# An attention-and-MLP block on one core: the front part laid out anew before the main loop

## The chip, the core and the metric

The kernel runs on one core of a Trainium2 chip, as one launch. The metric is the device time of that launch in microseconds. The engines are called as the profile calls them: PE (matrix products), DVE, ACT and POOL (elementwise work), SP (which here only issues transfers). PEld is PE's loading of weights.

## The reference, cut to what matters

```python
x = A_x                                               # 1 x 2048 x 512
mod = (silu(c) @ w_mod).reshape(1, 6, 1, 512)         # sa, ca, ga, sb, cb, gb
h = layernorm(x) * (1 + ca) + sa
q = (h @ wq), 32 heads of 16;  k = h @ wk;  v = h @ wv    # one key and value head for all
o = softmax(q @ k.T / 4) @ v
x = x + ga * (o @ wo)
h = layernorm(x) * (1 + cb) + sb
x = x + gb * (gelu(h @ w1 + b1) @ w2 + b2)            # 512 -> 1376 -> 512
```

## The kernel before, in words

**Two parts.** A front part loads x in four blocks of 512 rows, normalizes and modulates them, turns them so that features lie along partitions (the tiles h0 and big1 to big3, each as a high and a low part whose sum is the full number), and makes the keys and values of all 2048 rows. The main loop then runs over 64 units; a unit is 256 rows times 4 heads. For each unit the loop makes the scores of all keys (tile `e`, line 596), their exponentials on ACT (tile `p`, line 597) and the products with the values (tile `acc`, line 608). It also does, in pieces between these, the query projections of later groups, the output projection and the MLP.

**Maxima.** The softmax of a unit needs the maximum of each row of scores first. For this a score product `m` (line 516) of 128 rows times 512 keys goes into one of three PSUM banks, and DVE reduces it to one column of `mx` (line 521). A unit has 32 of them: key block kc 0 to 3, head pair j 0 or 1, row half t 0 or 1, and side s 0 or 1. The side says which half of PE's 128 rows the product uses: s = 0 the rows 0 to 63, s = 1 the rows 64 to 127. In the listings below a product is called m, then the unit, then j_t_kc_s. When the last maximum of a unit is in, `put_max` reduces the key blocks (tile `mm`, line 570), turns the result (`turned`, line 571), gathers it into `mt` (line 565), splits it into `mh` and `ml` and sends these with transfers (line 560) into two rows of the unit's query tile `qst`. Only then can the scores `e` of that unit be made. The maxima run ahead of the loop: those of unit 0 all come in the front part, with some of unit 1.

**What sets the order.** Every engine's order is written out by hand: the program is recorded in the order in which the Python code calls the operations. In the front part that order is the table `SLOTS`. Each row first does a number of maxima (`chunk`), then single steps of named jobs: "keys b" is three of the twelve products of the keys and values of block b (tile `kps`, line 163), and its fourth step also copies them out on ACT (`kv_out`, lines 391 and 392); "low b" is the low part of the keys on DVE (line 397); "k b" repeats them on ACT (line 401); "heads b" turns one quarter of block b (four transposes, tile `tp`, line 370) and modulates it; "v b" turns the values (tile `vps`); "q 1" is three products of the second query group (tile `qps`); "rows" is eight small products for the late modulation (tile `modl`); "wq g" splits the weights of query group g; "load" fetches the queries of unit 2. `FIRST_MAX` says in which order unit and key block of the first two units come, `LEAD_0` how many maxima (32 + 4 * LEAD_0) are done when the loop is entered. From there `lead` spreads what is left evenly over the first eight units.

**Transfers.** Query tiles go to DRAM (`send_q`) and come back into `qst` by four transfers for each unit (`load_q`, lines 486 and 487), all on SP's queue.

Of the kernel before, what the change touches and what calls it, by code (L numbers as in the profile page):

```python
# [22 lines left out]
LEAD_0 = 6  # L23
FIRST_MAX = ((0, 0), (1, 0), (0, 1), (1, 1), (0, 2), (0, 3), (1, 2), (1, 3))
SLOTS = ((4, "keys 1", "keys 1"), (2, "keys 1", "keys 1"), (2, "low 1", "heads 2"), (2, "heads 2", "k 1"), (2, "heads 2"), (2, "heads 2", "v 0"),
# [22 lines left out]
def raw(ap):  # L48
    return ap.bitcast(F32)
# [3 lines left out]
def adaln_mqa_mlp(  # L53
# [273 lines left out]
    def prep_wq(g):  # L327
        gs = slice(g * P, (g + 1) * P)
        for j in range(2):
# [3 lines left out]
            nc.scalar.copy(dh, src)  # L333
            nc.gpsimd.tensor_tensor(out=dl, in0=src, in1=raw(dh), op=ALU.subtract)
# [95 lines left out]
    def qproj(b, g):  # L430

        ps = psum.tile([P, BQ], F32, name=f"qps{b}_{g}", tag="v" if g else "x")
# [41 lines left out]
    def load_q(u):  # L474
# [7 lines left out]

        for s in (1, 0):
# [53 lines left out]
    def put_max(u, mx):  # L537
# [17 lines left out]
        def send():  # L555
            for s in (1, 0):
                for r, src in ((48, mh), (49, ml)):
                    dst = qst[64 * s + r:64 * s + r + 1].rearrange("p j (t n) -> p (j t) n", n=P)
                    ring = nc.scalar if u == 0 and s else nc.sync
# [3 lines left out]
        def gather():  # L563
            for g in range(0, P, 32):
                nc.gpsimd.tensor_scalar(out=mt[:, g:g + 32], in0=turned[g:g + 4 * T, :], scalar1=1.0, scalar2=0.0,  # L565
                                        op0=ALU.mult, op1=ALU.add)
            split(mh, ml, mt, nc.gpsimd, nc.gpsimd)
# [644 lines left out]
    def chunk(n):  # L1212
        for _ in range(n):
            mp.step(mp.done % 2)
# [53 lines left out]
    def one(fn, *args):  # L1268
        fn(*args)
        yield  # L1270
# [22 lines left out]
    def first_q(t):  # L1293
        if t == 1:
            run(q_group())
            load_q(0)
            load_q(1)
# [9 lines left out]

    def last_h(t):
        if t == QT - 1:
            run(h1)  # L1310
# [3 lines left out]
    repeat_k(0)  # L1314
    run(xhat1(2, act))
    run(xhat1(3, act))
    work = {"keys 1": keys(1), "heads 2": heads(2), "heads 3": heads(3), "q 1": q_group(), "keys 2": keys(2), "keys 3": keys(3),
# [215 lines left out]
```

## Time and profile before

| what | value |
|---|---|
| median of 3 runs | 1579.92 us (1579.86 to 1580.32) |
| the profiled execution | 1579.71 us, its span 1577.9 us |
| mean granted clock of PE | 0.997 |
| PE busy | 1554.7 us (99%) |
| DVE busy | 1403.8 us (89%) |
| ACT busy | 1204.3 us (76%) |
| POOL busy | 695.3 us (44%) |
| first score product `m` starts | 34.13 us |
| maxima of unit 0 complete (`mm` starts) | 74.03 us |
| first scores of the loop (`e` starts) | 79.75 us |

Times in the trace count from the start of the span. In a row of the timeline the first number is the start, the second the length, then engine, line and operation with its tiles; in brackets stands how long the engine idled before it and what the trace names as the end of that idle time. A row of the table by stretches gives the busy time and the number of instructions of PE, PEld, DVE, ACT and POOL, the granted clock of PE, and the transfers' share and rate.

### The profile page before, as it was taken

What the parts mean: (1) busy time and instruction counts of PE and PEld (TensorE: products, weight loads), DVE (VectorE), ACT (ScalarE), POOL (GpSimd) and SP (SyncE); (2) the same over time, 40 slices, a digit from 0 to 9 for tenths busy, and PEclk for the clock granted to TensorE, in tenths of its full rate; (3) what the DMA queues carried; (4) which work ended last, traced back from release to release, by engine and by line L of the source; (5) the groups of instructions that cost most, each with busy time, mean ns of one, the idle gap of its engine ahead of it and who ended that gap; (6) DMA issues with size and microseconds to landing.
All of it is one profiled execution on the core that took longest, in us unless ns stands there. A gap on an engine that the chain in (4) does not pass through costs nothing.

```text
span 1577.9 us, 43469 instructions
## 1 busy us (share of the span) xinstructions
PE 1554.7 (99%) x17506; PEld 1040.3 (66%) x17506; DVE 1403.8 (89%) x2491; ACT 1204.3 (76%) x2418; POOL 695.3 (44%) x1253
## 2 busy tenths in 40 slices
PE   5999999999999999999999999999999999999999
PEld 3466655667767676667766677676766677676767
DVE  6899999999999999999999999999999999999715
ACT  5477777788877887778877887778877788778863
POOL 4345447447422472245523463334712465224731
PEclk8999999999999999999999999999999999999999
DMA  7236323313021120312112130212112030221341
GB/s 250 83 110 203 121 81 91 100 36 105 20 61 63 59 82 22 93 33 94 46 44 83 44 99 19 76 48 86 56 32 93 27 107 31 62 76 49 100 141 54
DMA packets 80858, 121.48 MB, mean 77 GB/s; under 512 B 16186, under 2 KB 55354, under 8 KB 80400
## 3 DMA queue, kind: packets, MB, share of 16 engines
q1 hardware_dynamic: 80640, 118.70, 23.2%
q8 instruction: 137, 2.24, 0.6%
q14 instruction: 65, 0.53, 0.1%
q10 hardware_dynamic: 16, 0.00, 0.0%
HBM read 91.00 MB, written 26.88 MB: 75 GB/s over the span
## 4 chain that ended last, share of the span: by engine, by line
PE 95%; ACT 3%; DVE 1%; DMA 0%; issue 0%; POOL 0%; SPq 0%; ACTq 0%; DVEq 0%
PE acc L608 32%; PE e L596 20%; PE m L516 18%; PE w1ps L192 8%; PE w2ps L192 6%; PE wops L192 3%; PE qps L192 2%; ACT p L597 2%; PE w2ps L186 1%; PE w1ps L186 1%; PE tp L192 1%; DVE mx L521 1%; PE kps L163 1%; PE wops L186 0%; PE modr L288 0%; DMA xt<-in_A_x_dram 0%
## 5 line engine op out<-in xcount | busy, mean ns | idle before, releaser
L521 DVE TENSOR_REDUCE mx<-m 128x1 f32<-128x512 f32 x2048 | 1270.6, 681 | 98.9 <-PE m L516 90.3
L597 ACT ACTIVATE p<-e 128x512 f32<-128x512 f32 x2048 | 1067.1, 601 | 290.5 <-PE e L596 200.2
L516 PE MATMUL m<-ks,qst 64*128 64x512 f32 x2048 | 828.4, 431 | 6.4 <-DVE ve L204 4.9
L596 PE MATMUL e<-qst,ks 64*128 64x512 f32 x2048 | 731.5, 412 | 2.1 <-ACT wqH L333 1.3
L608 PE MATMUL acc<-p,va 128*32 128x256 f32 x8192 | 548.3, 385 | 0.0
L516 PEld LDWEIGHTS m<-ks,qst 64*128 64x128 f32 x2048 | 367.2, 184 | 103.4 <-DVE mx L521 82.2
L596 PEld LDWEIGHTS e<-qst,ks 64*128 64x128 f32 x2048 | 357.6, 184 | 112.6 <-ACT p L597 102.0
L608 PEld LDWEIGHTS acc<-p,va 128*32 128x32 f32 x8192 | 214.2, 109 | 216.9 <-issue 113.2
L192 PE MATMUL w1ps<-h2H,w1t 64*128 64x256 f32 x1232 | 236.1, 288 | 0.0
L192 PEld LDWEIGHTS w1ps<-h2H,w1t 64*128 64x128 f32 x1232 | 184.0, 185 | 31.7 <-issue 22.2
L565 POOL TENSOR_SCALAR mt<-turned 8x32 f32<-8x32 f32 x256 | 53.2, 208 | 339.0 <-DVE turned L571 326.9
L192 PE MATMUL w1ps<-h2L,w1t 64*128 64x256 f32 x616 | 169.3, 275 | 0.0
L192 PE MATMUL w2ps<-w2H,gH 64*128 64x256 f32 (+1 forms) x556 | 162.3, 296 | 0.0
L192 PE MATMUL w2ps<-w2L,gH 64*128 64x256 f32 (+1 forms) x556 | 156.6, 283 | 0.0
L192 PE MATMUL w2ps<-w2H,gL 64*128 64x256 f32 (+1 forms) x556 | 155.1, 283 | 0.0
L192 PEld LDWEIGHTS w1ps<-h2L,w1t 64*128 64x128 f32 x616 | 113.5, 184 | 0.0
L192 PEld LDWEIGHTS w2ps<-w2H,gH 64*128 64x128 f32 x556 | 101.6, 184 | 10.8 <-issue 4.9
L192 PEld LDWEIGHTS w2ps<-w2H,gL 64*128 64x128 f32 x556 | 101.8, 184 | 2.3
L192 PEld LDWEIGHTS w2ps<-w2L,gH 64*128 64x128 f32 x556 | 102.4, 184 | 1.4
L957 POOL TENSOR_SCALAR tt<-tt 128x256 f32<-128x256 f32 x77 | 31.0, 403 | 144.8 <-ACT tt L956 144.8
L192 PE MATMUL wops<-woH,onH 64*128 64x256 f32 x224 | 67.8, 303 | 0.0
L192 PE MATMUL wops<-woL,onH 64*128 64x256 f32 x224 | 62.2, 277 | 0.0
(233 smaller groups left out, 1602.7 us busy)
## 6 DMA issues: line engine op xcount, KB each, us to landing
w1t<-dw SPq DMA_DIRECT2D x82, 512.0 KB
qst<-dq SPq DMA_DIRECT2D x128, 64.0 KB
do<-oc SPq DMA_DIRECT2D x63, 128.0 KB
dw<-w1s SPq DMA_DIRECT2D x11, 512.0 KB
xt<-in_A_x_dram SPq DMA_DIRECT2D x4, 1024.0 KB
dq<-qH SPq DMA_DIRECT2D x16, 256.0 KB
dq<-qL SPq DMA_DIRECT2D x16, 256.0 KB
qst<-dq SPq DMA_DIRECT2D x128, 32.0 KB
```

What stands on the lines that cost most here:

```text
L163: nc.tensor.matmul(ps, a, b_, start=begin and n == 0, stop=end and n == last)
L186: nc.tensor.matmul(ps, a, b_, start=first_, stop=last_)
L192: nc.tensor.matmul(ps, a[rows], b_[rows], start=first_ and s == begin, stop=last_ and s != begin)
L516: nc.tensor.matmul(m, qsts[u][rows, j, t * P:(t + 1) * P], ks[rows, kc * 512:(kc + 1) * 512], start=True, stop=True)
L521: nc.vector.tensor_reduce(out=self.mx[u][:, i, kc:kc + 1], in_=m, axis=AX.X, op=ALU.max)
L565: nc.gpsimd.tensor_scalar(out=mt[:, g:g + 32], in0=turned[g:g + 4 * T, :], scalar1=1.0, scalar2=0.0, op0=ALU.mult, op1=ALU.add)
L596: nc.tensor.matmul(e, ks[rows, kt * P:(kt + 1) * P], rhs, start=True, stop=True)
L597: nc.scalar.activation(ptiles[u, K][:, j, s, :], e, AF.Exp, scale=0.25)
L608: ins = nc.tensor.matmul(accs[u][32 * cidx:32 * cidx + 32, :], va[:, kt, :], rhs, start=kt == 0, stop=kt == NKT - 1)
L957: nc.gpsimd.tensor_scalar(out=tt, in0=tt, scalar1=1.0, scalar2=1.0, op0=ALU.mult, op1=ALU.add)
```

## The change

- The second query group's twelve products and its evacuation move from the end of the front part to the time before the first maximum. The weights they need ("wq 1") are split on POOL instead of ACT and POOL, earlier. The group's PSUM tile changes its bank.
- `load_q` of the first two units fetches side 0 before side 1, and of each side the large part first.
- The first sixteen maxima come four of one side at a time, up to the fortieth two of one side at a time, then by turns.
- The normalization of block 3 ("x 3") moves from ACT to DVE, one quarter at a time between maxima.
- `FIRST_MAX` and `SLOTS` change: after the first key block's maxima of both units, those of unit 0 go on alone. In the slots of "keys 2" and "keys 3" there is mostly one maximum, where there were two. The heads of block 3 come after the keys of block 2.
- The gathering and splitting of unit 0's maxima moves from POOL to DVE. Of the transfers into `qst` that follow, side 0 instead of side 1 goes by ACT's queue.
- The loop is entered with 48 maxima done instead of 56 (`LEAD_0` 4 instead of 6). The eight others are done in the first eight units of the loop.

```diff
-LEAD_0 = 6
-FIRST_MAX = ((0, 0), (1, 0), (0, 1), (1, 1), (0, 2), (0, 3), (1, 2), (1, 3))
-SLOTS = ((4, "keys 1", "keys 1"), (2, "keys 1", "keys 1"), (2, "low 1", "heads 2"), ...
+LEAD_0 = 4
+FIRST_MAX = ((0, 0), (1, 0), (0, 1), (0, 2), (0, 3), (1, 1), (1, 2), (1, 3))
+SLOTS = ((4, "keys 1"), (2, "keys 1", "x 3"), (2, "keys 1", "x 3"), (2, "keys 1", "x 3"),
...
-    def prep_wq(g):
+    def prep_wq(g, eng=nc.scalar):
...
-            nc.scalar.copy(dh, src)
-            nc.gpsimd.tensor_tensor(out=dl, in0=src, in1=raw(dh), op=ALU.subtract)
+            split(dh, dl, src, eng, nc.gpsimd)
...
+        if u < 2:
+            for s in (0, 1):
+                low, high = (dq[h][g][part, a0 + s][:, :, cols] for part in (1, 0))
+                nc.sync.dma_start(out=raw(qst[64 * s + 16:64 * s + 48]), in_=high.unsqueeze(0).to_broadcast([2, 16, 2, w]))
+                nc.sync.dma_start(out=raw(qst[64 * s:64 * s + 16]), in_=low)
+            return
...
-                    ring = nc.scalar if u == 0 and s else nc.sync
+                    ring = nc.scalar if u == 0 and s == 0 else nc.sync
...
+            eng = nc.gpsimd if u else nc.vector
             for g in range(0, P, 32):
-                nc.gpsimd.tensor_scalar(out=mt[:, g:g + 32], in0=turned[g:g + 4 * T, :], scalar1=1.0, scalar2=0.0,
-                                        op0=ALU.mult, op1=ALU.add)
-            split(mh, ml, mt, nc.gpsimd, nc.gpsimd)
+                eng.tensor_scalar(out=mt[:, g:g + 32], in0=turned[g:g + 4 * T, :], scalar1=1.0, scalar2=0.0,
+                                  op0=ALU.mult, op1=ALU.add)
+            split(mh, ml, mt, eng, eng)
...
-            mp.step(mp.done % 2)
+            mp.step(mp.done // (4 if mp.done < 16 else 2 if mp.done < CH * (NKC + 1) else 1) % 2)
...
             run(q_group())
+            prep_wq(1, pool)
             load_q(0)
             load_q(1)
...
+    group = q_group()
+
     def last_h(t):
         if t == QT - 1:
+            run(h1, 1)
+            run(group, KD - 1)
             run(h1)
 
     stats1(3, last_h)
     load_mods(2)
     repeat_k(0)
+    run(group)
     run(xhat1(2, act))
-    run(xhat1(3, act))
```

PE, before the first maximum. Before the change the transposes of block 1 (`tp1`) are followed at once by the first four score products, whose sides alternate:

```order
L370 MATMUL tp1_2_406<-ident_75,xt1_145 128x128 x4
L370 MATMUL tp1_3_415<-ident_75,xt1_145 128x128 x4
L516 MATMUL m0_0_0_0_0_447<-ks_80,qst0_157 128x512
L516 MATMUL m0_0_0_0_1_450<-ks_80,qst0_157 128x512
L516 MATMUL m0_0_1_0_0_453<-ks_80,qst0_157 128x512
L516 MATMUL m0_0_1_0_1_456<-ks_80,qst0_157 128x512
L163 MATMUL kps1_459<-big1H_186,wkH_170 128x512
```

After the change the same place holds the second query group's products (`qps0_1`, nine ahead of the last four transposes and three behind), and the four score products are all of side 0:

```order
L165 MATMUL qps0_1_419<-h0H_192,wqL_183 128x512
L165 MATMUL qps0_1_419<-h0L_193,wqH_182 128x512
L371 MATMUL tp1_3_429<-ident_75,xt1_145 128x128 x4
L165 MATMUL qps0_1_419<-h0H_192,wqH_182 128x512
L165 MATMUL qps0_1_419<-h0H_192,wqL_183 128x512
L165 MATMUL qps0_1_419<-h0L_193,wqH_182 128x512
L523 MATMUL m0_0_0_0_0_468<-ks_80,qst0_157 128x512
L523 MATMUL m0_0_1_0_0_471<-ks_80,qst0_157 128x512
L523 MATMUL m0_1_0_0_0_474<-ks_80,qst0_157 128x512
L523 MATMUL m0_1_1_0_0_477<-ks_80,qst0_157 128x512
L165 MATMUL kps1_480<-big1H_186,wkH_170 128x512
```

So what stood at the end of the front part now stands ahead of the maxima. The next place is PE behind the products of the last key block (`kps3`). Before, four maxima of key block 2, the transposes of the values and the second query group follow them, ahead of the first maximum of key block 3 (`m0_0_0_3_0`):

```order
L163 MATMUL kps3_666<-big3L_191,wkH_170 128x512
L516 MATMUL m0_1_0_2_0_701<-ks_80,qst0_157 128x512
L516 MATMUL m0_1_0_2_1_704<-ks_80,qst0_157 128x512
L409 MATMUL vps2_709<-ident_75,vt2_644 128x32 x4
L516 MATMUL m0_1_1_2_0_715<-ks_80,qst0_157 128x512
L516 MATMUL m0_1_1_2_1_718<-ks_80,qst0_157 128x512
L163 MATMUL qps0_1_721<-h0H_192,wqH_182 128x512
L163 MATMUL qps0_1_721<-h0H_192,wqL_183 128x512
L163 MATMUL qps0_1_721<-h0L_193,wqH_182 128x512
L516 MATMUL m0_0_0_3_0_725<-ks_80,qst0_157 128x512
```

After the change the maximum of key block 3 follows at once:

```order
L523 MATMUL m0_1_1_2_1_700<-ks_80,qst0_157 128x512
L165 MATMUL kps3_684<-big3H_188,wkH_170 128x512
L165 MATMUL kps3_684<-big3H_188,wkL_171 128x512
L165 MATMUL kps3_684<-big3L_191,wkH_170 128x512
L523 MATMUL m0_0_0_3_0_716<-ks_80,qst0_157 128x512
L523 MATMUL m0_0_1_3_0_719<-ks_80,qst0_157 128x512
L410 MATMUL vps2_722<-ident_75,vt2_609 128x32 x4
```

Nothing stands between the last key product and the first maximum that needs the key block any more. The third place is DVE when the last maximum of unit 0 is in. After the change the gathering (`mt`, `mh`, `ml`) stands on DVE between it and the next reductions; before, `turned` was followed at once by the next reduction, and POOL gathered:

```order
L528 TENSOR_REDUCE mx0_467<-m0_1_1_3_1_753 128x1
L578 TENSOR_REDUCE mm0_756<-mx0_467 128x8
L579 STREAM_TRANSPOSE turned0_760<-mm0_756 128x32
L573 TENSOR_SCALAR mt0_763<-turned0_760 8x32 x4
L137 CAST mh0_764<-mt0_763 8x128
L140 TENSOR_TENSOR ml0_765<-mt0_763,mh0_764 8x128
L528 TENSOR_REDUCE mx1_504<-m1_0_0_1_0_778 128x1
```

So the reductions that follow now wait behind seven small DVE operations. In the loop, a half step is what lies between two groups of `acc` products. Each has four score products and four `e`; after the change eight of the first 64 half steps have five score products.

More of the change, by code (lines that the diff above doesn't have):

```diff
@@ L22 @@
 LEAD = 6
-LEAD_0 = 6
-FIRST_MAX = ((0, 0), (1, 0), (0, 1), (1, 1), (0, 2), (0, 3), (1, 2), (1, 3))
-SLOTS = ((4, "keys 1", "keys 1"), (2, "keys 1", "keys 1"), (2, "low 1", "heads 2"), (2, "heads 2", "k 1"), (2, "heads 2"), (2, "heads 2", "v 0"),
[4 rows of a table removed]
+LEAD_0 = 4
+FIRST_MAX = ((0, 0), (1, 0), (0, 1), (0, 2), (0, 3), (1, 1), (1, 2), (1, 3))
+SLOTS = ((4, "keys 1"), (2, "keys 1", "x 3"), (2, "keys 1", "x 3"), (2, "keys 1", "x 3"),
[5 rows of a table added]
+         (2, "rows"), (2, "rows", "load"), (2, "rows", "rows"), (2, ))
 MAX_WAIT = (1, 4)
@@ L430, in qproj @@
     def qproj(b, g):
-        ps = psum.tile([P, BQ], F32, name=f"qps{b}_{g}", tag="v" if g else "x")
+        ps = psum.tile([P, BQ], F32, name=f"qps{b}_{g}", tag="x")
         yield from mm3(ps, qpairs(b, g), 3, 1)
@@ L1314, in adaln_mqa_mlp @@
     repeat_k(0)
+    run(group)
     run(xhat1(2, act))
-    run(xhat1(3, act))
-    work = {"keys 1": keys(1), "heads 2": heads(2), "heads 3": heads(3), "q 1": q_group(), "keys 2": keys(2), "keys 3": keys(3),
+    work = {"keys 1": keys(1), "heads 2": heads(2), "heads 3": heads(3), "x 3": xhat1(3, dve), "keys 2": keys(2), "keys 3": keys(3),
             "v 0": one(v_out, 0), "v 1": one(v_out, 1), "v 2": one(v_out, 2), "v 3": one(v_out, 3), "rows": late_rows(),
             "low 1": one(low_k, 1), "low 2": one(low_k, 2), "low 3": one(low_k, 3), "k 1": one(repeat_k, 1), "k 2": one(repeat_k, 2), "k 3": one(repeat_k, 3), "load": one(load_q, 2),
-            "wq 1": one(prep_wq, 1), "wq 2": one(prep_wq, 2), "wq 3": one(prep_wq, 3)}
+            "wq 2": one(prep_wq, 2), "wq 3": one(prep_wq, 3)}
     for n, *names in SLOTS:
```

9 rows, old and new, of the table SLOTS are left out of this document.

## The prediction

> **What bounds the kernel.** I read the head of the page first, then the table by stretches for the first 126 us, then the timelines of PE, DVE and ACT through the front part.
>
> ```profile
> span 1577.9 us, 43469 instructions
> ...
> PE 1554.7 (99%) x17506; PEld 1040.3 (66%) x17506; DVE 1403.8 (89%) x2491; ACT 1204.3 (76%) x2418; POOL 695.3 (44%) x1253
> ```
>
> ```profile
> 50.00:60.00 10.00, 10.00 (x47) 5.88 (x47) 9.31 (x16) 6.30 (x10) 7.00 (x7) 1.00 0.21 88
> 60.00:70.00 10.00, 9.68 (x36) 4.81 (x35) 9.46 (x16) 4.12 (x9) 1.45 (x2) 1.00 0.00 0
> 103.00:126.00 23.00, 23.00 (x243) 14.41 (x242) 21.22 (x37) 17.19 (x34) 12.91 (x18) 1.00 0.57 193
> ```
>
> In the loop (last row) PE has no free time and DVE 8%. From 50 us on PE and DVE are both over 93% busy in the front part too; PE's slack lies before, from about 28 to 35 us, as the next table shows. So filling the early hole is worth something only as far as DVE can use it, and work handed to the loop costs PE time there.
>
> The same table cut at the instants where the granted clock (the eighth number) changes shows a second cost of the hole:
>
> ```profile
> 28.08:31.49 3.41, 0.66 (x4) 0.42 (x4) 3.12 (x6) 3.35 (x6) 2.61 (x6) 1.00 0.14 33
> 31.49:34.90 3.41, 0.77 (x3) 0.50 (x3) 1.93 (x7) 3.33 (x6) 2.29 (x2) 0.50 0.47 84
> 34.90:38.32 3.42, 3.06 (x8) 1.82 (x7) 2.48 (x4) 3.42 (x6) 0.66 (x3) 0.50 0.89 312
> 38.32:41.73 3.41, 3.41 (x9) 2.03 (x8) 1.29 (x2) 0.62 (x1) 0.00 (x0) 0.50 1.03 412
> 75.86:79.28 3.42, 2.57 (x20) 0.53 (x12) 3.07 (x6) 1.07 (x5) 0.99 (x3) 1.00 0.07 12
> ```
>
> The clock is halved from 31.49 to 41.73, three stretches of 3.41 us. A stretch with 0.66 us of work was followed by the half clock, one with 3.06 kept it, one with 3.41 ended it, and the one of 75.86, with 2.57, did no harm. Between 0.66 and 2.57 no row decides.
>
> **The rows for the sum.** They are from the timelines; rows between them are left out. PE first:
>
> ```profile
> 34.13 1.19 PE L516 MATMUL m<-ks,qst 64*128 64x512 f32 x3 [4.87 <-DVE ve L204]
> 39.26 0.79 PE L516 MATMUL m<-ks,qst 64*128 64x512 f32 x2
> 39.98 0.79 PE L163 MATMUL kps<-big1H,wkH 128*128 128x512 f32 x1
> 47.92 0.43 PE L409 MATMUL vps<-ident,vt 32*128 32x32 f32 x4
> 49.98 0.66 PE L370 MATMUL tp<-ident,xt 128*128 128x128 f32 x4
> 50.57 0.68 PE L516 MATMUL m<-ks,qst 64*128 64x512 f32 x2
> 53.65 0.49 PE L516 MATMUL m<-ks,qst 64*128 64x512 f32 x2
> 54.07 0.51 PE L163 MATMUL kps<-big2H,wkH 128*128 128x512 f32 x1
> 54.98 0.49 PE L516 MATMUL m<-ks,qst 64*128 64x512 f32 x2
> 67.15 0.47 PE L516 MATMUL m<-ks,qst 64*128 64x512 f32 x1 [0.32 <-DVE mx L521]
> 67.55 0.50 PE L163 MATMUL qps<-h0H,wqH 128*128 128x512 f32 x1
> 76.94 1.06 PE L288 MATMUL modl<-wml,csb 128*32 128x512 f32 x8
> 77.93 0.49 PE L516 MATMUL m<-ks,qst 64*128 64x512 f32 x2
> 79.75 0.59 PE L596 MATMUL e<-qst,ks 64*128 64x512 f32 x2 [1.32 <-ACT wqH L333]
> 83.69 1.07 PE L608 MATMUL acc<-p,va 128*32 128x256 f32 x16
> 90.83 0.39 PE L596 MATMUL e<-qst,ks 64*128 64x512 f32 x1
> 91.06 0.39 PE L516 MATMUL m<-ks,qst 64*128 64x512 f32 x1
> ```
>
> One row of the chain that ended last, key products at the half clock:
>
> ```profile
> 36.47 2.86 PE kps L163 x6
> ```
>
> DVE, then ACT and POOL:
>
> ```profile
> 11.28 1.92 DVE L363 TENSOR_SCALAR xt<-xt,mv,rs 128x512 f32<-128x512 f32 x4 [1.15 <-POOL rs L206]
> 33.92 0.17 DVE L204 TENSOR_SCALAR ve<-mv 128x4 f32<-128x4 f32 x1
> 34.93 2.48 DVE L521 TENSOR_REDUCE mx<-m 128x1 f32<-128x512 f32 x4 [0.85 <-PE m L516]
> 48.81 4.87 DVE L521 TENSOR_REDUCE mx<-m 128x1 f32<-128x512 f32 x8 [0.17 <-PE m L516]
> 65.60 0.68 DVE L397 TENSOR_TENSOR ks<-kps,ks 16x512 fp32r<-16x512 f32 x1
> 66.31 2.48 DVE L521 TENSOR_REDUCE mx<-m 128x1 f32<-128x512 f32 x4
> 74.03 0.19 DVE L570 TENSOR_REDUCE mm<-mx 128x8 f32<-128x32 f32 x1
> 74.25 0.21 DVE L571 STREAM_TRANSPOSE turned<-mm 128x32 f32<-128x32 f32 x1
> ```
>
> ```profile
> 63.81 1.17 ACT L391 CAST ks<-kps 48x512 fp32r<-48x512 f32 x2 [1.96 <-PE kps L163]
> 71.88 0.62 ACT L133 CAST qH<-q 128x512 fp32r<-128x512 f32 x1
> 14.19 1.55 POOL L334 TENSOR_TENSOR wqL<-wqf,wqH 128x256 fp32r<-128x256 f32 x2 [2.94 <-ACT wqH L333]
> 27.16 1.01 POOL L206 TENSOR_TENSOR rs<-ve,mhalf 128x4 f32<-128x4 f32 x1 [4.48 <-DVE ve L204]
> ```
>
> Read from starts, not lengths: two score products of different sides and the switch back to key products take 54.07 - 53.65 = 0.42; a single one takes 67.55 - 67.15 = 0.40, nearly as much, so the two of a pair run side by side. Two of one side cannot: in the loop, products on one side follow each other at 91.06 - 90.83 = 0.23, so I take 0.42 + 0.23 = 0.65 for such a pair. Three key products take 54.98 - 54.07 = 0.91, four transposes 50.57 - 49.98 = 0.59, eight `modl` 0.99. A reduction takes 4.87 / 8 = 0.61, a quarter of a block's normalization on DVE 1.92 / 4 = 0.48. After key products the first maximum of that key block waits 66.31 - 63.81 = 2.5: ACT's copies, then DVE's low part.
>
> **The sum through the front part.** DVE's work up to `ve` is the same in both orders, so its first reduction comes no earlier than 34.1 (34.93 before): moving the query group ahead opens PE's time, not DVE's. From there, at full clock:
> - Keys 1: DVE needs 4 x 0.61 + 3 x (2 x 0.61 + 0.48) = 7.5, PE less, 1.31 + 3 x (0.65 + 0.91) = 6.0 from 34.8. To 41.6.
> - Heads 2: six maxima, low keys 0.7 and a last quarter 0.48 on DVE, 4.8; PE about the same. To 46.4.
> - Keys 2: one maximum to three key products, PE 4 x (0.40 + 0.91) = 5.2, with DVE half idle. To 51.6.
> - Heads 3: PE 0.40 + 3 x 0.65 + 4 x 0.59 + 0.43 for the values = 5.1, and 0.8 of waiting, since DVE stands at the low keys of block 2 and three banks are full. To 57.5.
> - Keys 3: 0.65 + 0.91 + 3 x 1.31 = 5.5. To 63.0.
> - The 2.5 us for the last key block now have no query group under them: 65.5. This is the wait that takes the place of the early hole.
> - Eight maxima of key block 3: 8 x 0.61 + 0.5 = 5.4. Unit 0 is complete at 70.9, where it was at 74.03.
> - To the first `e`: PE has four pairs and 32 `modl`, 4 x 0.42 + 4 x 0.99 = 5.7, of which about 1.2 is issued ahead of `mm`. DVE's gathering (six operations near the 0.21 of `turned`, about 1.6 with what stands ahead) stops the reductions that free PE's banks, so up to 1.6 is added: 4.5 to 6.1, and I take the middle, 5.3, where the trace has 79.75 - 74.03 = 5.7. First `e` at 76.2.
>
> So at full clock the front part ends 79.75 - 76.2 = 3.5 us earlier.
>
> **The clock.** PE would run the query group until about 31, then three score products (the fourth needs a freed bank, 34.1 + 0.7), so the stretch from 31.49 to 34.90 holds some 0.8 us of work. That is nearest to the row with 0.66, so I expect the half clock from 34.90. With it six key products take 2.86 (the row of the chain), three so 1.43, and a pair of one side 39.98 - 39.26 + 0.43 = 1.15: 2.6 a slot against DVE's 1.7. A stretch then does 1.3 slots instead of 2, which loses 0.7 x 1.7 = 1.2 us. PE would be busy throughout it, as in the row with 3.41, so I take one stretch: +1.2; two would be +2.4.
>
> [...]
>
> **The loop.** Eight half steps get a fifth score product. In a half step the side with the score products has four of them and three `e` and decides, so one more costs 0.23: +1.84. Were PE to balance the sides, it would be half, +0.92; DVE has 23.00 - 21.22 = 1.8 us free in a unit and takes 0.61 more in it, so DVE adds nothing I can see. I take 1.84.
>
> **The rest at no cost.** Splitting "wq 1" on POOL: two subtractions 1.55 and two casts, at most as long again, 3.1 in the 4.48 that POOL idles before 27.16, done about when the products want them, at 27.4; what came later would push the query group, which DVE doesn't wait for, by as much. The group's evacuation puts a copy and a cast on ACT, 0.62 each, ahead of block 2's normalization, needed only at heads 2, about 42. SP: the new order of `load_q` brings side 0 earlier than the 34.13 of the trace by two issues; two more transfers of queries pass the modulation's loads, which nothing needs before 70. ACT's queue still carries one side's two transfers; the first `e` follows PE's own work there.
>
> **Sum.** 1579.71 - 3.5 + 1.2 + 1.84 = 1579.2; the median lies 0.2 above the profiled execution: **1579.4 us**, in effect no change. What a measurement of this kernel can tell from none is about 0.2%, 3.2 us.
>
> **The rivals.**
> - The clock stays up: -3.5 + 1.84, **1578.2**. For it: PE works on until 31 and its gaps are half as long; against it the 0.8 us in the stretch. [...]
> - Two stretches at half clock: **1580.6**. For it: the row with 3.06, which was not enough.
> - Slower: the wait of 2.5 us behind the last key block is a new hole, which holds PE to about 1 us of work in a stretch of 3.41. If the limit lies above that, the clock falls there as well and is still down at the end: 32 `modl` take 4.0 more, of which 1.6 fill waits, and the first unit's 83.69 - 79.75 = 3.9 takes 1.7 more, together +4.1: **1583.5**. It decides if a stretch that is a third busy cools. Against it: 2.57 did not.
> - The loop absorbs the eight maxima and the clock stays up: -3.5, **1576.4**. For it DVE's and ACT's free time; against it PE's 23.00 of 23.00.
>
> **Chances.** One stretch 0.35, clock up 0.30, two stretches 0.14, the loop absorbs 0.12, the second fall 0.09. Faster by over 0.2% is the absorbing case, with a little of its neighbour: 0.13. Slower by over 0.2% is the second fall: 0.08. Within it 0.79. The range leaves out the outer halves of these two: 1576.7 to 1581.8.
>
> **What would show it.** First reduction near 34.1; the query group between 27 and 31; a clock of 0.50 in one stretch from about 34.9 and none at 28; DVE idle 2 us or more before the first maximum of key block 3; `mm` near 72; first `e` near 77; the eight half steps 0.2 longer. The prediction is wrong if reductions start well before 34, if the wait behind the last keys is covered, or if DVE holds PE up in the loop.

## The result: slower by 1.5%, where no change was forecast

| kernel | median us | runs | ratio to before, 95% interval |
|---|---|---|---|
| before | 1579.89 (1578.71 to 1580.32) | 4 | |
| after the change | 1602.59 (1601.42 to 1604.50) | 4 | 1.0146 (1.0128 to 1.0164) |

The forecast was 1579.4 within 1576.7 to 1581.8; the time lies 20.8 us above that range. The predicted mechanism came: the clock fell in the early hole. But it stayed down for 65 us, where one stretch of 3.4 us was expected.

**The profile after.** The line of the granted clock on the page shows it at once (40 slices of 40 us; the second slice has half clock throughout):

```profile
PEclk9579999999999999999999999999999999999999
```

The table by stretches of the kernel after, cut at the edges of the clock. Columns as in the prediction: PE, PEld, DVE, ACT and POOL busy, then the clock:

```profile
29.64:33.05 3.41, 1.22 (x5) 0.48 (x3) 2.50 (x6) 3.30 (x6) 2.70 (x3) 1.00 0.40 67
33.05:36.46 3.41, 2.21 (x4) 1.11 (x4) 2.87 (x9) 3.38 (x6) 2.65 (x4) 0.50 0.96 278
36.46:39.88 3.42, 3.42 (x8) 1.83 (x7) 1.74 (x3) 0.17 (x1) 0.00 (x0) 0.50 1.02 387
56.94:60.36 3.42, 3.42 (x8) 1.58 (x6) 0.78 (x2) 0.00 (x0) 0.00 (x0) 0.50 0.00 0
94.49:97.90 3.41, 3.41 (x18) 0.52 (x16) 1.29 (x2) 0.00 (x0) 0.00 (x0) 0.50 0.69 195
97.90:101.32 3.42, 3.03 (x19) 1.53 (x15) 2.81 (x5) 2.97 (x6) 0.00 (x0) 1.00 0.26 77
33.05:97.90 64.85, 60.77 (x159) 28.86 (x159) 35.66 (x66) 22.54 (x40) 17.27 (x22) 0.50 0.25 86
```

The clock falls at 33.05, behind a stretch with 1.22 us of busy time, and rises at 97.90, nineteen stretches later. In fifteen of these nineteen PE counts as busy from edge to edge (three of the rows shown), and only behind the last of them does the clock rise; DVE, which was over 93% busy from 50 us on before, is busy for 35.66 of 64.85 us. So PE at half clock sets the pace of the whole front part. The rows of PE and DVE in one slot of "keys 2" show how:

```profile
56.23 0.79 PE L165 MATMUL kps<-big2H,wkH 128*128 128x512 f32 x1
56.82 0.63 PE L165 MATMUL kps<-big2H,wkL 128*128 128x512 f32 x1
57.25 0.63 PE L165 MATMUL kps<-big2L,wkH 128*128 128x512 f32 x1
57.80 0.79 PE L523 MATMUL m<-ks,qst 64*128 64x512 f32 x1
58.53 0.79 PE L165 MATMUL kps<-big2H,wkH 128*128 128x512 f32 x1
```

```profile
58.64 0.69 DVE L528 TENSOR_REDUCE mx<-m 128x1 f32<-128x512 f32 x1 [1.61 <-PE m L523]
```

A slot takes 58.53 - 56.23 = 2.30 us where the prediction had 1.31, and DVE idles 1.61 us in each. Consecutive key products start 57.25 - 56.82 = 0.43 apart, so four products stream for 1.72 of 2.30 us; the rest goes with the two changes between score and key products. "Busy" in the table covers these changes as well.

The wait behind the last key block, `mm`, the first `e` and the first `acc` after the change:

```profile
81.87 1.22 PE L523 MATMUL m<-ks,qst 64*128 64x512 f32 x2 [2.57 <-DVE ks L398]
98.31 0.39 PE L604 MATMUL e<-qst,ks 64*128 64x512 f32 x2
102.67 1.07 PE L616 MATMUL acc<-p,va 128*32 128x256 f32 x16
```

```profile
88.70 0.18 DVE L578 TENSOR_REDUCE mm<-mx 128x8 f32<-128x32 f32 x1
```

The spans differ by 1601.6 - 1577.9 = 23.7 us. Of these 102.67 - 83.69 = 19.0 have come together by the first `acc`, and 4.7 come after it, in the loop.

### The profile page after: what moved, and what is told of

Its sections match the earlier page's. It is cut to its first block, busy times and chain, and to the rows that moved or that the text cites. A ratio compares the mean times of both kernels' runs of the same rounds, so it can differ in the third digit from the quotient of the medians.

```text
span 1601.6 us, 43499 instructions
## 1 busy us (share of the span) xinstructions
PE 1579.1 (99%) x17506; PEld 1049.1 (66%) x17506; DVE 1407.5 (88%) x2501; ACT 1200.3 (75%) x2412; POOL 695.0 (43%) x1249
## 4 chain that ended last, share of the span: by engine, by line
PE 94%; ACT 2%; DVE 1%; DMA 1%; issue 0%; POOL 0%; SPq 0%; DVEq 0%; ACTq 0%; POOLq 0%
PE acc L616 31%; PE m L523 19%; PE e L604 19%; PE w1ps L194 8%; PE w2ps L194 6%; PE wops L194 3%; PE qps L194 2%; ACT p L605 2%; PE w2ps L188 1%; PE kps L165 1%; DVE mx L528 1%; PE w1ps L188 1%; DMA xt<-in_A_x_dram 1%; PE tp L194 1%; PE tp L371 1%; PE modl L290 0%
## 5 line engine op out<-in xcount | busy, mean ns | idle before, releaser
L523 PE MATMUL m<-ks,qst 64*128 64x512 f32 x2048 | 841.6, 436 | 7.3 <-DVE mx L528 3.0
L523 PEld LDWEIGHTS m<-ks,qst 64*128 64x128 f32 x2048 | 371.9, 186 | 113.9 <-DVE mx L528 89.2
```

The lines of the kernel that those rows point to most:

```text
L523: nc.tensor.matmul(m, qsts[u][rows, j, t * P:(t + 1) * P], ks[rows, kc * 512:(kc + 1) * 512], start=True, stop=True)
```

## The experiments

All idle products come from one small function, put into both kernels; its result is never read:

```diff
+    def fill(n, tag, rows=P):
+        ps = psum.tile([P, BQ], F32, name=f"fill_{tag}", tag=tag)
+        for _ in range(n):
+            nc.tensor.matmul(ps, wkH[:rows, 0, :], wkH.rearrange("p k n -> p (k n)")[:rows], start=True, stop=True)
```

Ratios are to the kernel before on the same chip (medians there 1578.8 to 1580.3). Each run was traced once, so where the clock fell is known for one execution of it; of the others only the mean granted clock is on record.

### Is it the clock, and what brings it back?

**The early hole filled** (e1), all slots left as they are:

```diff
     for i, (n, *names) in enumerate(SLOTS):
-        chunk(n)
+        if i == 0: chunk(n - 1); fill(11, "v"); chunk(1)
+        else: chunk(n)
```

> The changed kernel with 11 idle key-sized products (128 rows by 512 columns, result unused) between its third and fourth score product, where PE waits for DVE from 31.6 to 34.25 us. Theory A (the loss is the half clock alone: the hole drops it, and the new order, which changes between score and key products after every one to three products, never fills a stretch of 3.41 us well enough to get it back): no half clock after 30 us, first e near 76 us instead of 98.3, and 1602.6 - 22 = 1580 to 1582, since the loop's part of the loss (about 4.7 us) stays. Rival C (the new order itself is slow, by waits between PE and DVE, and the clock only goes with it): first e stays above 85 us and the time above 1588.

Measured: 1586.19 us (1585.14 to 1589.77), ratio 1.0051 (1.0036 to 1.0066). The changed kernel stood 22.7 us above the kernel before, this one 7.4 above it on its own chip, so 15.3 us are gone. The clock stayed whole to 65.25 us, as theory A has it, and then fell, where the rival "slower" of the prediction had put it. Theory A had no second fall, and its 1580 to 1582 and first `e` near 76 (measured 80.64) were missed; the 1588 and 85 us of rival C weren't reached either. Table by stretches, and PE's row behind the last key product, of this run:

```profile
51.60:55.01 3.41, 2.46 (x13) 1.36 (x13) 2.25 (x4) 3.30 (x6) 0.09 (x1) 1.00 0.01 2
61.84:65.25 3.41, 1.11 (x4) 0.48 (x3) 1.17 (x2) 1.74 (x3) 0.00 (x0) 1.00 0.00 0
65.25:78.91 13.66, 13.08 (x42) 5.04 (x46) 9.98 (x23) 2.41 (x7) 3.29 (x8) 0.50 0.04 10
```

```profile
65.52 1.22 PE L528 MATMUL m<-ks,qst 64*128 64x512 f32 x2 [2.56 <-DVE ks L403]
```

Up to the first maximum of key block 3 the slots ran as the prediction had summed them for a whole clock: it said 65.5, the row says 65.52.

**A burst of 17 idle products in the halved part** (e2), and the same with 64 of the 128 rows (e3); both ahead of the third slot, the second with `rows=64`:

```diff
     for i, (n, *names) in enumerate(SLOTS):
+        if i == 2: fill(17, "x", 128)
         chunk(n)
```

> The changed kernel with 17 idle products of 128 rows in one row ahead of its third slot (about 39.3 us), where the clock is halved: 7.3 us at half clock, so that at least one whole stretch of 3.41 us is filled without a break. Theory A (share of the time in which products stream) and rival B (share of the array's rows in use): the clock is whole again from between 42 and 47 us, first e near 83, time 1585 to 1591. Rival C (PE's waits decide, not a stretch): the clock stays halved to about 100 us and the time rises by the burst, to 1607 to 1611.

> As the run with the burst of 128 rows, but the 17 idle products use 64 of the 128 rows, as a score product of one side does, and take as long. Theory A (what counts is the share of the time in which products stream, however many rows they use): the clock comes back as there, time 1585 to 1591. Rival B (what counts is how much of the array is in use; score products of one side leave half of it idle): half the rows are 0.5, below the 0.6 to 0.7 with which the clock stayed halved, so it stays halved to about 100 us and the time is 1607 to 1611.

Measured: 1597.61 with 128 rows and 1606.08 with 64 (one run each; the kernel before 1578.81). The stretch that the burst fills, and the next, first with 128 rows, then with 64:

```profile
39.90:43.31 3.41, 3.41 (x9) 2.64 (x8) 0.00 (x0) 0.00 (x0) 0.00 (x0) 0.50 0.96 323
43.31:46.73 3.42, 3.42 (x14) 2.01 (x12) 1.13 (x2) 0.00 (x0) 0.00 (x0) 1.00 0.07 25
```

```profile
41.20:44.62 3.42, 3.42 (x10) 2.62 (x9) 0.00 (x0) 0.00 (x0) 0.00 (x0) 0.50 0.73 276
44.62:48.03 3.41, 3.41 (x11) 2.36 (x10) 0.71 (x2) 0.00 (x0) 0.00 (x0) 0.50 0.03 12
```

The first stretch of each streams without a break. With all rows the clock rose at once, with half of them it did not. Theory A, by which the time of streaming counts, is wrong; rival B, by which the share of the array in use counts, holds, with one execution of each. The time with 128 rows missed the 1585 to 1591, since the clock fell again at 63.80, among the heads of block 3, and stayed down to 91.10. With 64 rows the clock came back at 78.75, earlier than the 100 expected, and fell again at 85.58.

**Twelve key products in one row** (e4), and **sides by turns** (e5):

```diff
-SLOTS = ((4, "keys 1"), (2, "keys 1", "x 3"), (2, "keys 1", "x 3"), (2, "keys 1", "x 3"),
+SLOTS = ((4, "keys 1", "keys 1", "keys 1", "keys 1"), (2, "x 3"), (2, "x 3"), (2, "x 3"),
```

```diff
-            mp.step(mp.done // (4 if mp.done < 16 else 2 if mp.done < CH * (NKC + 1) else 1) % 2)
+            mp.step(mp.done % 2)
```

> The changed kernel with all twelve products of key block 1 in one row behind the first four score products (SLOTS rows 1 to 4: (4, keys 1 x4), (2, x 3) x3), nothing idle added. Theory A: twelve products stream for 12 x 0.43 = 5.1 us at half clock with one break ahead of them, which fills a stretch of 3.41 us to over 0.83 wherever its edges lie, or nearly so; the clock is whole again by 45 us, first e 77 to 81, time 1581 to 1585. If twelve in a row are not enough, the clock stays halved and the time stays near 1602. Rival C: 1595 or more, since the order of the rest is the same.

> The changed kernel with the sides of the score products by turns from the first one on, as before the change, all else as changed. A pair then runs side by side and uses all rows. Rival B as it stands after the bursts (the clock comes back after a stretch in which more than about three quarters of the array's rows stream): in the slots of key block 1 a pair and three key products stream 4 x 0.43 = 1.72 of 2.3 us with all rows, 0.75, right at that mark, so the clock comes back early, between 38 and 50 us, and the time is 1585 to 1595, with a second fall behind the last keys. If it stays halved to 75 us or more, the side order is not what keeps it down, and the time is 1597 to 1603.

Measured for twelve in a row: 1601.58, ratio 1.0137 (1.0120 to 1.0154), hardly better, far from the 1581 to 1585 of theory A and in the range of rival C. The clock did rise, at 41.16, as theory A has it, and fell after one stretch, because the slots behind held score products alone:

```profile
37.75:41.16 3.41, 3.41 (x9) 2.27 (x8) 0.00 (x0) 0.33 (x1) 0.00 (x0) 0.50 1.03 401
41.16:44.57 3.41, 2.35 (x7) 0.91 (x6) 3.12 (x6) 1.41 (x3) 0.00 (x0) 1.00 0.85 339
44.57:95.77 51.20, 47.96 (x132) 23.38 (x136) 29.01 (x52) 17.26 (x31) 14.63 (x18) 0.50 0.07 24
```

The fatal stretch has 2.35 us of busy PE, about as much as the 2.57 that the prediction took for harmless. Measured for the sides by turns: 1596.57 (one run), 1.6 above the expected 1585 to 1595; the clock came back at 64.69, later than the 38 to 50 expected, so it stayed halved for 30.7 us at first where the changed kernel had 64.9, and it fell again at 74.94, behind the last keys. Pairs side by side put more of the array to use in less time (two score products of different sides took 0.79 us at half clock before the change, two of one side 1.22 after it), which helped here and was not enough.

**The kernel before with three key products to a pair** (e15), as the changed one has them:

```diff
-SLOTS = ((4, "keys 1", "keys 1"), (2, "keys 1", "keys 1"), (2, "low 1", "heads 2"), (2, "heads 2", "k 1"), (2, "heads 2"), (2, "heads 2", "v 0"),
+SLOTS = ((4, "keys 1"), (2, "keys 1"), (2, "keys 1"), (2, "keys 1"), (2, "low 1", "heads 2"), (2, "heads 2", "k 1"), (0, "heads 2"), (0, "heads 2", "v 0"),
```

> The kernel before with one thing of the change: the key products of block 1 stand three to a pair of score products instead of six (two slots of heads 2 give up their score products in turn); sides by turns, group at the end, all else as before. Theory (a stretch must keep about 0.8 of the array's rows streaming to raise the clock; six in a row and a pair do, 0.83, three and a pair do not, 0.75): the clock falls at 31 to 35 us as before and comes back only with the transposes and pairs or later, 48 to 65 us; time 3 to 8 us above before, ratio 1.002 to 1.005. Rival (what kept it down were the single and one-sided score products, not the spreading): back within 14 us, ratio 0.999 to 1.001.

Measured: 1582.54 (1578.76 to 1586.21), ratio 1.0013 (0.9999 to 1.0026): a loss of about 2 us, not clear of no change, and between the theory and its rival. In the profiled execution, with 1585.76 one of the slowest of the ten, the half clock lasted from 31.37 to 48.43, five stretches instead of three, which is the theory's direction; the clock fell twice more there, at 68.91 and 85.98, for two stretches each. So the spreading goes with a longer halved part, in one execution, but does not make 65 us. What is left are the single score products, the one-sided pairs (e5) and the normalization on DVE; how much each has, these runs don't say.

### The mark, from all the runs

For each stretch of 3.41 us between 20 and 100 us of all nineteen traces I took each product's streaming time (512 columns: 0.43 us at half clock, as the key products show, and half of that at full, where the trace has them 0.23 apart; `modl` and `acc`, which use 32 of 128 columns of the array, twice that, as if four ran side by side, since eight `modl` take 90.64 - 88.78 = 1.86 us at half clock), times the share of the array it uses by its row in the timeline (64*128 is half of 128*128), and divided the sum by 3.41. So the uses are estimates. Stretches with transposes are left out, since it isn't plain how they count: 126 of 448, with 7 of the 27 falls and 5 of the 27 rises.

| what the clock did behind the stretch | use of the array | share of time streaming |
|---|---|---|
| whole, fell (20 stretches) | 0.04 to 0.35 | 0.08 to 0.54 |
| whole, stayed so | 0.38 and more | 0.43 and more |
| halved, stayed so | up to 0.73, and two of 0.77 and 0.79 | up to 1.00 |
| halved, rose (22 stretches) | 0.74 to 1.00 | 0.78 and more |

By use of the array the four groups part almost cleanly; by time of streaming they overlap widely. So in these stretches a whole clock fell behind uses up to 0.35 and stayed behind 0.38 and more, and a halved one rose only behind 0.74 and more. Busy time says little: in e7 the clock fell behind a stretch with 3.36 us of busy PE and a use of 0.33, mostly score products of 64 rows:

```profile
64.33:67.75 3.42, 3.36 (x18) 1.89 (x16) 2.82 (x5) 2.06 (x7) 1.43 (x2) 1.00 0.00 0
```

For the changed order this gives, slot by slot: a pair of one side and three key products at half clock come to (3 x 0.43 + 2 x 0.43 / 2) / 2.73 = 0.63, a single score product and three key products to (3 + 0.5) x 0.43 / 2.30 = 0.65: the changed order lies between the two marks nearly everywhere. Once halved, the clock stayed halved for 64.85 us; only the sixteen `modl` at its end, 0.98, ended it.

### What the order is worth at a whole clock

**Both holes filled** (e6: 11 more idle products behind the last key product), and **the same with 56 maxima at the loop's entry** (e7: `LEAD_0 = 6`):

```diff
+        if "low 3" in names: fill(11, "v")
```

> The run with the filled hole, with 11 more idle products of 128 rows behind the last product of key block 3 (2.5 us, where PE waits for the copies and the low part). The hole there dropped the clock at 65.25 us in that run. Theory: with both holes filled no half clock at all, first e at 76 to 77 us, as the prediction had it for the clock that stays up; from the first acc product to the end some 4 us longer than before the change (measured 3.8 and 4.7); together 1578.8 - 3.5 + 4.3, 1579 to 1581. If the front part itself brings nothing, first e is above 78.5 and the time above 1582.

> The same with 56 maxima at the loop's entry instead of 48 (LEAD_0 = 6): the eight others are done at the end of the front part. Theory (a fifth score product stands alone in its half step at 0.40 to 0.43 us, and delays what waits for the maxima): from the first acc product to the end it is again 1494.2 us as before the change, 4 us less; the front part gets longer by at most 8 x 0.61 = 4.9 us, less what DVE idles there now; so 1578 to 1580.5. Rival (the loop's loss comes from the changed order of units or transfers, not from the eight): that part stays at 1498 or more, and the time is 1583 to 1586.

Measured: 1587.42, ratio 1.0051 (1.0035 to 1.0067), and 1586.65, ratio 1.0049 (1.0032 to 1.0065). In neither did the clock stay whole: in the profiled execution of e6, the slowest of its six, it fell at 45.70, behind heads 2, and at 79.83, of e7 at 67.75 and 84.82. So both expected times, 1579 to 1581 and 1578 to 1580.5, were missed, because I had taken the two holes for the only thin places. Two things can still be read from e7, whose clock was whole up to 67.75. Unit 0 was complete at 70.59, where the prediction had 70.9:

```profile
70.59 0.19 DVE L583 TENSOR_REDUCE mm<-mx 128x8 f32<-128x32 f32 x1
```

```profile
88.74 1.93 PE L621 MATMUL acc<-p,va 128*32 128x256 f32 x16
```

And its loop, from the first `acc` at 88.74 to the end of the span at 1582.62, took 1582.62 - 88.74 = 1493.9 us, against 1577.92 - 83.69 = 1494.2 before the change; the ten traces with 48 maxima have 1498.1 to 1500.1. So the eight maxima cost 4 to 6 us in the loop, as this expectation's theory has it, and not its rival (the order of units or transfers). The fifth product stands alone. First rows of PE from a half step of the changed kernel and from a later one, then the lengths of two half steps with five, and of one with four from before the change (last row):

```profile
122.47 0.43 PE L523 MATMUL m<-ks,qst 64*128 64x512 f32 x1
122.50 0.40 PE L604 MATMUL e<-qst,ks 64*128 64x512 f32 x1
122.86 0.50 PE L523 MATMUL m<-ks,qst 64*128 64x512 f32 x1
123.29 1.07 PE L616 MATMUL acc<-p,va 128*32 128x256 f32 x16
...
169.63 0.46 PE L604 MATMUL e<-qst,ks 64*128 64x512 f32 x1 [0.86 <-DMA qst<-ml]
```

```profile
119.98:123.29 3.31, 3.31 (x34) 1.95 (x32) 2.92 (x5) 2.51 (x6) 0.88 (x1) 1.00 0.41 116
123.29:126.58 3.29, 3.29 (x32) 1.89 (x31) 3.07 (x6) 2.46 (x7) 0.00 (x0) 1.00 0.32 115
```

```profile
101.01:103.87 2.86, 2.86 (x33) 1.81 (x31) 2.49 (x5) 2.07 (x5) 0.91 (x1) 1.00 0.38 100
```

The fifth has no `e` of the other side beside it, so it costs 123.29 - 122.86 = 0.43, not 0.23. And the maxima of the next units are complete later: the `mm` of unit 3 stands 159.73 - 102.67 = 57.1 us behind the first `acc`, before the change 133.90 - 83.69 = 50.2, and that unit's first `e`, the row of 169.63, waits 0.86 us for their transfer.

**All thin places filled** (e13: also two idle products in each slot of heads 2 and in four slots behind the last keys; e16: in the first two slots of heads 3 and ahead of the first `e` as well):

```diff
+        if "heads 2" in names or i in (12, 13): fill(2, "x")
+        elif i in (21, 22, 23, 24): fill(2, "v")
...
+    fill(5, "v")
```

> The changed kernel with both holes filled as before, and two idle products more in each of the four slots of heads 2 and in four slots behind the last keys, where DVE sets the pace and the clock fell in the earlier runs. Theory: the clock stays whole in most executions to the last wait before the first e; the sum of the prediction holds for the front part (first e at 76 to 78 us), and the loop's part is 4 to 4.7 us longer than before the change; together 1579.5 to 1582, no gain. If the order as such is slow, first e is above 80 us with a whole clock.

> The changed kernel with both holes, the slots of heads 2, the first two of heads 3, four slots behind the last keys and the wait ahead of the first e filled with idle products. Theory: the clock is whole up to the loop, first e at 77 to 79 us (the prediction's 76.2, and 0.5 us for each place where the filling itself takes PE longer than the wait it fills), the loop's part 4 to 4.7 us longer; together 1580 to 1583. If the order is slow as such, first e comes above 80 us with a whole clock.

Measured: 1590.01, ratio 1.0052 (1.0034 to 1.0071), with the clock down from 56.22 to 69.87, behind the wait of 0.95 us in the first row below; and with the last gaps filled 1587.10 (1586.28 to 1587.71), ratio 1.0045 (1.0030 to 1.0060), with a whole clock through the front part. First PE's row of e13, then the table by stretches of e16 and two of its rows of PE:

```profile
55.62 0.47 PE L528 MATMUL m<-ks,qst 64*128 64x512 f32 x1 [0.95 <-ACT big3H L135]
```

```profile
34.14:81.92 47.78, 46.30 (x200) 23.84 (x199) 35.89 (x63) 21.87 (x40) 17.06 (x22) 1.00 0.29 102
```

```profile
75.92 0.49 PE L528 MATMUL m<-ks,qst 64*128 64x512 f32 x1 [1.10 <-DVE mx L533]
81.44 0.49 PE L609 MATMUL e<-qst,ks 64*128 64x512 f32 x2
```

e13 missed its expectation, since its clock fell. In e16 the mean granted clock was 1.0 in all four executions, and yet the first `e` stands at 81.44: the sign that the expectation names for an order that is slow as such came. The filling itself takes part of it: `mm` came at 73.51, 2.9 later than in e7, and five idle products (1.1 us) stand ahead of `e`. Taking both off leaves 1583.1 as an estimate, still 3 us more than before. So by this estimate the changed order would not gain even with a whole clock; no run shows it with a whole clock and without the fillings.

### Single parts, and the kernel before without its hole

**The kernel before with its hole filled** (e8), **and the wait ahead of the first `e`** (e11), **and two products in heads 2** (e17):

```diff
+        if i == 0: fill(20, "v")       # e8, e11, e17
+        if i == 4: fill(2, "x")        # e17
         chunk(n)
...
+    fill(5, "v")                       # e11, e17, behind the slots
```

> The kernel before with 20 idle products of 128 rows (4.5 us) ahead of its first score product, where PE idles from 29.3 to 34.1 us; nothing else. Theory: its three halved stretches (31.5 to 41.7 us) go; first reduction 0.3 earlier; DVE idles 3.1 us in the two later stretches, of which the most comes back: first e 77 to 78 instead of 79.75, time 1576 to 1577.5 against 1578.8. Rival (DVE sets the front part there, so the clock costs nothing): 1578.3 to 1579.2.

> The kernel before with the early hole filled by 20 idle products, and 5 more (1.1 us) behind the last score product before the loop, where PE waits 1.3 us for the transfer of the maxima and where the clock fell at 78.9 us in the run with the early hole filled. Theory: no half clock in most executions; first e 76.7 as there, the first unit 0.3 to 0.6 shorter; time 1575.5 to 1576.5, and less spread than 1575.5 to 1580.7. Rival (that fall came from what lies behind, the first unit's own products): the clock falls all the same, 1576.8.

> The kernel before with the early hole and the wait ahead of the first e filled, as in the run of ratio 0.9979, and two idle products more in the slots of heads 2, where PE waits 0.57 us for a bank. Theory: that place was whole in that run but near the mark, so little is gained: ratio 0.997 to 0.9985, no execution above 1579. Rival (the products in that wait delay the score products behind them): 0.9985 to 1.

Measured: 1576.80, ratio 0.9985 (0.9975 to 0.9994); 1577.26, ratio 0.9979 (0.9970 to 0.9988); 1577.31, ratio 0.9982 (0.9973 to 0.9992). All three are 2 to 3 us under the kernel before, and their intervals overlap, so the runs don't tell them apart; the times of e8 and e17 came as expected, and e11 lies above its 1575.5 to 1576.5 on a chip where the kernel before took 1580.09. In the trace of e11, without half clock, `mm` and first `e` come 2.7 us earlier than before the change (74.03, 79.75):

```profile
71.29 0.19 DVE L575 TENSOR_REDUCE mm<-mx 128x8 f32<-128x32 f32 x1
```

```profile
77.00 0.59 PE L601 MATMUL e<-qst,ks 64*128 64x512 f32 x2
```

71.29 is within 0.7 of the 70.59 of e7: most of what the new order was to bring to unit 0 is what the old one has at a whole clock. The third filling adds nothing clear: two of its ten executions took 1579.0 and 1579.2, at the edge of what was expected, and in the traced one the clock fell at 63.24, at a place not filled.

**The early query group alone** (e10), **the same with fillings** (e14), **and the gathering on DVE alone** (e12, on top of e11):

```diff
+            prep_wq(1, pool)                    # e10, e14: behind the first query group
+            run(group, KD - 1)                  # and the group as after the change
-         (0, "v 2"), (2, "q 1"), (2, "q 1"), (2, "q 1"), (2, "q 1", "rows"),
+         (0, "v 2"), (2, ), (2, ), (2, ), (2, "rows"),
+            eng = nc.gpsimd if u else nc.vector # e12: in gather(), as after the change
```

> The kernel before with this one part of the change alone: the second query group and the split of its weights stand ahead of the first score product, and its slots at the end hold score products alone. Theory: the group ends by 30 us and does not reach over the wait for the first score product (34.1), so the clock still falls, near 31 to 35 us, and comes back with the six key products in a row, within 14 us; at the end the slots hold a pair of score products in 1.2 us of DVE's time, a share of the array of 0.2 to 0.4, so it falls a second time between 65 and 72 us and stays down for 7 to 14 us; time 1581 to 1587. Rival (moving the group alone gains, as it takes 3 us of products out of the later front part): 1576 to 1579.

> The kernel before with the second query group ahead of the first score product, 13 idle products between the two, three in each of four slots at the end, and five ahead of the first e. Theory: the clock is whole; the group's 2.8 us are out of the later front part, where PE was the bound, so mm comes at 69 to 70.5 us instead of 71.0 to 71.3 and first e at 75 to 76.5; 1 us less than the kernel before with idle products alone (ratio 0.9979): ratio 0.997 to 0.998. Rival (DVE sets the later front part, so the group's place is worth nothing): ratio 0.998 to 0.9985.

> The same with one more part of the change: the first unit's maxima are gathered and split on DVE instead of POOL. From the start of mm to the first transfer's issue it took 1.94 us with POOL and 1.49 with DVE in the runs so far; first e 0.45 earlier if only that chain ends last, and unchanged if DVE's later reductions, which wait 1.3 us, hold up PE's last score products as long. Expected 0 to 0.4 us less than the run without it.

Measured for the group alone: 1580.46, ratio 0.9998 (0.9989 to 1.0008), no change, where 1581 to 1587 was expected. Both falls of the expectation are there in the trace, and a short one at 47.12 besides, 20.5 us of half clock where the kernel before has 10.2; the loss that was to come of them isn't, and what made up for it these runs don't show:

```profile
30.05:33.46 3.41, 0.47 (x3) 0.29 (x3) 2.51 (x8) 3.30 (x6) 2.60 (x3) 1.00 0.21 69
33.46:40.29 6.83, 6.43 (x15) 3.59 (x15) 4.06 (x9) 6.28 (x10) 2.65 (x4) 0.50 0.97 326
64.18:67.59 3.41, 2.18 (x9) 0.93 (x7) 3.30 (x6) 2.01 (x5) 0.00 (x0) 1.00 0.00 0
67.59:77.83 10.24, 10.24 (x38) 3.18 (x38) 7.25 (x14) 0.00 (x0) 1.56 (x6) 0.50 0.01 2
```

The group does not reach over the wait for the first score product, so the clock falls as before; and where it stood, the slots now hold score products alone and the clock falls there too. With fillings (e14) 1579.69, ratio 0.9991 (0.9981 to 1.0000), above what theory and rival had: the clock fell at 43.45 in the profiled execution, a place not filled, and its mean was 0.996 to 0.998 in all ten. Nothing was gained over filling alone, and what the early group is worth at a whole clock stays open. The gathering on DVE: 1581.46, ratio 0.9999 (0.9987 to 1.0010), where 0 to 0.4 us less than e11 was expected; it takes back the whole gain of e11. In the traced execution PE waits for DVE's reductions behind the gathering, and `mm` to first `e` takes 77.86 - 70.91 = 6.95 us instead of 77.00 - 71.29 = 5.71:

```profile
73.32 0.50 PE L521 MATMUL m<-ks,qst 64*128 64x512 f32 x1 [1.14 <-DVE mx L526]
```

This wait is the smaller part of the loss. The traced execution had a whole clock and was, with 1577.37, the fastest of the ten, 0.5 us above the traced one of e11. Six of the others took 1581.45 to 1582.45 with a mean granted clock of 0.996 or 0.997, so most of the loss goes with half clock; where it came, and whether by the new wait, isn't on record.

**The group back at the end of the changed kernel** (e9), early hole filled: 1595.07, ratio 1.0092 (1.0070 to 1.0115), far above the 1580.5 to 1583.5 expected.

> The changed kernel with one part undone: the second query group stands again at the end, six of its products in the wait behind the last key product and three each in the next two slots, the late rows one slot earlier; the early hole, which it leaves, is filled with 9 idle products ahead of the first score product and 11 after the third. Theory (the group was what kept the array in use behind the last keys, and its move to the front let the clock fall there): no fall between 60 and 68 us, where the run with the filled hole alone fell, first e 77 to 80, the loop's part 4 longer than before as in all runs with 48 maxima; time 1580.5 to 1583.5. It may still fall in a thin slot between 40 and 60 us, where some edge cuts it badly (1586 and more). If the clock falls at 65 us just the same, the group is not the cover.

This run tells nothing of its question. I had put the weights' split "wq 2" ahead of the group in the same slot, and the group waited for it on ACT instead of covering the wait, so the clock fell at 68.51:

```profile
67.00 0.51 PE L165 MATMUL qps<-h0H,wqH 128*128 128x512 f32 x1 [3.27 <-ACT wqH L135]
```

## Why the prediction was wrong

**The step that failed** is the one on the length of the half clock: "PE would be busy throughout it, as in the row with 3.41, so I take one stretch: +1.2". The busy time of a stretch is not what raised the clock in these runs: after the change fifteen halved stretches had PE busy from edge to edge, and it rose behind the last alone. The row with 3.41 had six key products and a pair side by side, a use of 0.83; the predicted slots have 0.63. From the prediction's own numbers (three key products 0.43 apart, one-sided pair, 2.6 a slot) that could have been worked out, but I had no mark to hold it against and took the only recovery that the trace showed for the rule. Filling the first hole alone took the excess over the kernel before from 22.7 us to 7.4. With the later falls the half clock accounts for about 1602.6 - 1587.1 = 15.5 us as e16 measured with its fillings, and for about 1602.6 - 1583.1 = 19.5 by the estimate above for a whole clock.

**The same mistake stands in the row of 75.86:** "2.57, did no harm" was read as busy time. By use of the array that stretch has 0.53, thanks to `modl`, while the one of e4 with 2.35 us of score products alone has 0.17, and the clock fell behind it.

**Idle gaps.** In e1 the gap in which the clock fell at 65.25 is 2.56 us long, the one ahead of 56.22 in e13 is 0.95, and in e7 the stretch ahead of 67.75 has only 0.06 us of idle PE; in e16 the clock stayed whole over a gap of 1.10 (row of 75.92). So in these runs the length of a gap doesn't tell whether the clock falls. Nor does PE's busy time tell when it rises: after the change the clock stayed down through fourteen stretches with PE busy from edge to edge, and in e3 through one that streamed without a break on half the rows.

**The loop.** "One more costs 0.23: +1.84" was mis-sized: 4.7 us in the profiled execution, 4 to 6 over the runs. The 0.23 is the distance of products that follow each other on one side while the other side works; the fifth stands alone at 0.43, in eight half steps 3.4 us, and the first `e` of unit 3 waits 0.86; together 4.3 of the 4.7.

**From `mm` to the first `e`.** Forecast 5.3 (4.5 to 6.1); 81.44 - 73.51 - 1.1 = 6.8 in e16. DVE's gathering (six operations: `mt` four times, `mh`, `ml`) held PE for 1.10, within the 1.6 that was priced; the rest stands in the products behind.

**Right were** the early reduction (33.50 against 34.1), the group between 26.5 and 30, the fall in the hole, the wait of 2.5 us behind the last keys (2.57), and the sum of the slots at a whole clock: 65.52 against 65.5 in e1, 70.59 against 70.9 in e7, the last 2.8 us of it at half clock. The gain of 3.5 us that I drew from it, though, needs a whole clock throughout, and the kernel before gets most of it by filling its own hole.

**Of the rivals**, the second fall behind the last key block had 0.09 and came as soon as the clock was whole there (e1, e3, e5). No case stood for a half clock that lasts, though the row with 3.06, "which was not enough", spoke for it.

## What to carry to other kernels

Judge a stretch of PE's time by the share of the array that streams, not by its busy time: in these runs the clock halved behind stretches of 3.41 us with a use up to 0.35 and came back only behind those with 0.74 and more, so slots between the two, like those of the changed order with 0.63 and 0.65, kept whatever clock they had. When work is moved out of a slot to fill a hole, ask what it leaves there. A few idle products in a hole are a cheap test of what the clock costs, and may be the better change (0.9979 here).

## What the runs showed of the hardware

- The clock kept its state: one slot of "keys 2" took 50.24 - 48.93 = 1.31 us with a whole clock (e16, rows below) and 2.30 with a halved one, in the same order, and the halved one lasted 64.85 us after the change, up to the sixteen `modl` with 0.98.

```profile
48.93 0.50 PE L528 MATMUL m<-ks,qst 64*128 64x512 f32 x1
50.24 0.49 PE L528 MATMUL m<-ks,qst 64*128 64x512 f32 x1
```

- Half the rows didn't count in full: 3.42 us of unbroken products of 64 rows left the clock halved (e3, 41.20 to 44.62); one stretch of 128 rows raised it (e2, 39.90 to 43.31).
- The edges are 3.41 us apart (97.90 - 33.05 = 64.85 is nineteen of them, 41.73 - 31.49 = 10.24 three) and don't lie alike in the traces: in the early hole the clock fell at 31.49 us before the change, at 33.05 after it and at 33.98 in e5. The order with thin stretches spread in time: 1585.0 to 1593.5 over six runs of e6, the slowest with a mean granted clock of 0.989 and the others with 0.994 to 0.997, against 1578.2 to 1581.8 over fifteen of the kernel before on the same chip. That the place of the edges makes the spread is likely, not shown.
